# A wider padding tile under the experts' operand blocks: 256 bytes instead of 128

## The chip, the cores and the metric

The kernel runs on one core of a Trainium2 chip. The metric is the device time of one execution in microseconds (us); single matmuls are given in nanoseconds (ns). The engines are called as the profile calls them: PE is TensorE's matmul, PEld its weight load (the load of a matmul's stationary operand), DVE is VectorE, ACT is ScalarE, POOL is GpSimd, SP is SyncE, which issues most of the DMAs.

## The reference

Two stages follow each other. An attention over 8 batches, 8 heads, 576 positions and 64 values a head is the sum of a coarse attention over positions averaged by four and of a local one over a narrow band. Its output, 4608 tokens of 512 values, goes into a mixture of eight experts, in which every token goes to one expert:

```python
def _moe_ref(x, modality_id, w_gate, modality_bias, w1, w2):
    logits = x @ w_gate + modality_bias[modality_id]
    e_idx = np.argmax(logits, axis=1)
...
    gate_w = probs[np.arange(N), e_idx]
    for e in range(E):
        mask = e_idx == e
...
        h = np.maximum(x[mask] @ w1[e], 0.0)
        out[mask] = gate_w[mask, None] * (h @ w2[e])
```

Here w1 is 8 x 512 x 1024 and w2 is 8 x 1024 x 512, all in float32.

## The kernel before

**Two halves.** The first 238 us compute the attention and, with it, the routing: tokens are sorted by expert into a table in DRAM. From there on the kernel is a row of expert products, and the change touches only these.

**Units.** The loop over `order` (in `build`) goes through eight units of rows of one expert each: two of 512 rows (the early ones, "e"), three of 1024 rows ("q", class `Large`), then one of 256, one of 128 and one of 256 rows ("m"). A loop at the end takes what is left over, and on these inputs it runs no round. Every unit has a first product (rows by w1, then relu) and a second (hidden rows by w2, then a scale by the gate, then an indirect DMA to the output). Each number of an operand is split in two, a high part and a low part, and each product is three matmuls: high by high, low by high, high by low.

**Blocks.** An operand lives in a block of 8192 bytes in each of the 128 partitions: a high half and a low half of 4096 bytes, or, for rows of a unit of 512, one block for the high part and one for the low. `Moe.block` (the function that hands them out by name) takes them from pools. G0 and G1 come from the pool `xg`; G2, G3, H0 to H3, V2, V3 and raw2 from `mxb`; H4 and H5 from `mwa`; raw0 and raw1 from `mwr`. H6, H7, X0, X1, V0 and V1 come from `mwe`, which `open_early` opens on the right side, that is at the upper end of the memory:

```python
        s.we = ctx.enter_context(s.tc.tile_pool(name="mwe", bufs=1, side="right", reuse_waits="tile"))
```

A tile `pad` that nothing reads or writes is asked of this pool last, in `build`, just ahead of the loop over what is left. The pool ends at the memory's upper end, so the size of its last tile sets where the six blocks before it begin.

**Who meets whom on PE.** In a matmul one operand is stationary (loaded by PEld, 128 columns of 4 bytes) and one is moving (512 columns of 4 bytes, 256 in the first products of the units of 256 rows). Which blocks meet, by the code:

- Early units, first product (`compute`, L1003): weights in H4, H5, H6, H7 are stationary, rows in X0 and X1 are moving. 96 matmuls each, half of them with H4 and H5, half with H6 and H7.
- Early units, second product (`second`, L1057): hidden rows in H0 to H3 are stationary, weights in V0 to V3 are moving. 96 matmuls each.
- Large units, first product (`Large.first`, L1171): seven smaller products (three of eight are saved by sums, after Strassen and Winograd), whose operand blocks `Large.WHERE` lists, rows first, weights second. Of the first large unit:

```python
    WHERE = ({"1": "G0 G1", "2": "G2 G3", "5": "H4 H5", "6": "H6 H7", "7": "G0 G1", "4": "G2 G3", "3": "G0 G1"},
```

- In the other large units H2, H3, H0 and H1 stand in for H4 to H7, and for G0 to G3 in part. 168 matmuls a unit, 24 in each of the seven products. The raw rows, not yet split, are in X0 and X1, and only DVE, ACT and POOL read them there.
- Large units, second product (`second`, L1057): 192 matmuls a unit, 24 for each h of 0 to 7. In the first 12 of an h the moving weights are V0 and V1, in the last 12 V2 and V3. The hidden rows are stationary: for h of 0 to 3 H0 and H1 in the first 12 and H2 and H3 in the last 12, for h of 4 to 7 H4 and H5 and then H6 and H7.
- Units of 256 rows, first product (L1003): 96 matmuls each, weights in G and H blocks stationary, rows in X0 or X1 moving with 256 columns.
- Unit of 128 rows: first product (`compute_half`, L1025), 24 matmuls, rows in X stationary, weights in V0 to V3 moving; second product (L1057), 24 matmuls.

**What sets the order.** PE's order comes from the loops of `compute`, `Large.first` and `second` and from the framework's scheduler, which may put a ready matmul ahead; a unit's splits of weights and rows on ACT, DVE and POOL and the loads on SP's queue are hooked onto the matmuls, several to an h. Weights come as raw blocks over SP's queue (`fetch`, L849 and L852), are split by `wsplit` (L874 on ACT, L880 on DVE) or by `Large.split` (L1120 and L1121), rows come by indirect DMA on POOL's queue (L935) into `xg` tiles and are turned by PE (L963).

Of the kernel before, what the change touches and what calls it, by code (L numbers as in the profile page):

```python
# [7 lines left out]
F32 = mybir.dt.float32  # L8
# [1187 lines left out]
def build(tc, q, k, v, mid, w_gate, bias, w1, w2, out):  # L1196
    nc = tc.nc
    with ExitStack() as ctx:
# [9 lines left out]
        moe = Moe(tc, ctx, C, ps, xs, tab, w1, w2, out)  # L1208
# [350 lines left out]
                else:  # L1559
                    moe.compute(Ts[i], Ws[i], Xs[i], H, paced, mid, Js.get(i), i == N - 1)  # L1560

        moe.we.tile([128, 32], F32, name="pad")
        rbi, rei = ro.rest()
        nu = nc.values_load(rei[0:1, NLOOP : NLOOP + 1], min_val=0, max_val=NLOOP)  # L1564
        moe.after = ()
# [40 lines left out]
```

## Time and profile before

| what | value |
|---|---|
| median of 3 runs | 667.25 us (660.24 to 670.42) |
| profiled execution, whole time | 660.17 us |
| profiled execution, span of its instructions | 658.1 us |
| PE busy | 630.8 us, 96% of the span |
| DVE, ACT, POOL busy | 437.5, 384.4 and 341.9 us |
| DMA | 90.21 MB, mean 137 GB/s |

The span runs from the first to the last instruction of the core; the execution's own time has 2.1 us around it. A group of PE in the profile is 390 ns long for one matmul of 512 columns, since matmuls overlap; what one costs in a stream is the distance between the starts of neighbours.

### The profile page before, as it was taken

The page shows a single profiled execution, that of the slowest core. Times are in us where ns is not written, and L with a number is a line of the kernel's source. Part 1 is how long each engine was busy: PE and PEld are TensorE (multiplying, and loading weights), DVE is VectorE, ACT ScalarE, POOL GpSimd, SP SyncE. Part 2 cuts the span into 40 slices and gives each one's busy share as a digit, 9 for nine tenths or more (in the row PEclk, how much of TensorE's full clock was granted, in tenths as well). Part 3 has the DMA queues.
Part 4 walks back from the last instruction along what each step waited for, and adds up shares of the span by engine and source line. Part 5 has one row for each costly group of instructions (what it writes and reads, how often), then busy time and mean ns, then how long its engine had stood idle before and what let it go on. Part 6 is the DMA issues. An engine that isn't in the chain of part 4 may idle for free. (4 is left out here: it accounts for less than half of the span.)

```text
span 658.1 us, 16392 instructions
## 1 busy us (share of the span) xinstructions
PE 630.8 (96%) x6099; PEld 495.7 (75%) x6099; DVE 437.5 (66%) x896; ACT 384.4 (58%) x870; POOL 341.9 (52%) x378
## 2 busy tenths in 40 slices
PE   9899999999998889998999999999999999999996
PEld 5677676666766667876888788887888878889794
DVE  6689898899988866933456754567548775246610
ACT  4689989988998863212545623456234574245610
POOL 6644564745557861515078775588755721141211
PEclk9899999998999999999999999999999999999998
DMA  8999997899989975498012454134431345349300
GB/s 191 205 188 195 175 183 149 159 182 147 176 162 149 195 200 154 82 179 207 17 35 100 106 140 117 49 97 109 124 136 49 101 119 173 121 151 289 125 15 32
DMA packets 168860, 90.21 MB, mean 137 GB/s; under 512 B 131812, under 2 KB 153354, under 8 KB 168778
## 3 DMA queue, kind: packets, MB, share of 16 engines
q1 hardware_dynamic: 160810, 69.96, 50.3%
q0 software_dynamic: 7968, 19.18, 9.6%
q8 instruction: 49, 0.80, 0.6%
q14 instruction: 33, 0.27, 0.2%
HBM read 69.86 MB, written 19.51 MB: 136 GB/s over the span
## 5 line engine op out<-in xcount | busy, mean ns | idle before, releaser
L1057 PE MATMUL l<-V,H 128*128 128x512 f32 x792 | 187.2, 394 | 0.0
L1057 PEld LDWEIGHTS l<-V,H 128*128 128x128 f32 x792 | 148.0, 188 | 33.9
L943 POOL DMA_INDIRECT xg<-xs,m x64 | 77.0, 1204 | 19.2 <-issue 18.9
L426 POOL TENSOR_TENSOR le<-le,zr 128x384 f32<-128x384 f32 x32 | 26.6, 832 | 78.0 <-DVE zr L422 40.9
L1067 POOL DMA_INDIRECT out_dram<-o,tq x24 | 27.4, 1140 | 74.6 <-ACT o L1059 55.8
L1003 PE MATMUL l<-X,H 128*128 128x512 f32 (+1 forms) x240 | 54.2, 375 | 2.8 <-ACT o L1059 1.8
L442 ACT COPY Pw<-lt 32x288 f32<-32x288 f32 x128 | 54.6, 427 | 1.6
L1059 ACT ACTIVATE o<-l,tq 128x512 f32<-128x512 f32 x24 | 16.6, 690 | 66.5 <-issue 27.8
L640 POOL DMA_INDIRECT tab<-ig,si x36 | 36.8, 1022 | 26.1 <-DVE mni L662 18.1
L1003 PEld LDWEIGHTS l<-X,H 128*128 128x128 f32 x240 | 41.5, 188 | 11.3 <-ACT o L1059 2.2
L1160 ACT ACTIVATE H<-o 128x512 fp32r<-128x512 f32 x36 | 22.8, 634 | 39.6 <-DVE o L1182 30.2
L331 ACT COPY kT<-tp 64x512 f32<-64x512 f32 x64 | 37.2, 581 | 8.9 <-PE tp L294 7.4
L481 PEld LDWEIGHTS avl<-Pw,vw 128*64 128x64 f32 x768 | 32.7, 137 | 10.9 <-ACT Pw L442 3.4
L481 PE MATMUL avl<-Pw,vw 128*64 128x96 f32 x768 | 38.8, 250 | 2.2 <-ACT Pw L442 2.2
L1067 POOL DMA_INDIRECT out_dram<-o,tg x10 | 11.3, 1132 | 52.9 <-ACT o L1059 35.8
L880 DVE TENSOR_TENSOR V<-raw,V 128x1024 fp32r<-128x1024 f32 x22 | 31.8, 1467 | 10.2 <-ACT V L874 9.1
L1121 DVE TENSOR_TENSOR G<-X,G 128x1024 fp32r<-128x1024 f32 x15 | 23.2, 1551 | 22.3 <-ACT G L1120 16.1
L1009 DVE SCALAR_TENSOR_TENSOR H<-l,H 128x512 fp32r<-128x512 f32 x24 | 16.1, 686 | 32.7 <-ACT H L1008 28.6
L412 ACT ACTIVATE de<-scd,dm 128x144 f32<-128x144 f32 x96 | 35.2, 373 | 1.7 <-DVE dm L404 0.4
L373 PE MATMUL sc<-kT,qT 128*24 128x64 f32 x1536 | 35.1, 224 | 0.4 <-ACT qT L318 0.3
L1008 ACT ACTIVATE H<-l 128x512 fp32r<-128x512 f32 x24 | 13.9, 596 | 35.9 <-PE l L1003 27.8
L373 PEld LDWEIGHTS sc<-kT,qT 128*24 128x24 f32 x1536 | 24.7, 104 | 12.9 <-issue 10.5
(282 smaller groups left out, 1437.6 us busy)
## 6 DMA issues: line engine op xcount, KB each, us to landing
raw<-in_moe_w_dram SPq DMA_DIRECT2D x112, 128.0 KB
raw<-in_moe_w_dram SPq DMA_DIRECT2D x28, 512.0 KB
vw<-in_v_dram SPq DMA_DIRECT2D x60, 180.0 KB
qt<-in_q_dram SPq DMA_DIRECT2D x26, 288.0 KB
kt<-in_k_dram SPq DMA_DIRECT2D x26, 288.0 KB
xs<-R SPq DMA_DIRECT2D x48, 128.0 KB
xs<-G SPq DMA_DIRECT2D x16, 128.0 KB
qt<-in_q_dram SPq DMA_DIRECT2D x6, 256.0 KB
```

The source lines that it names most:

```text
L331: s.nc.scalar.copy(s.kB[r, g, a, PAD + 64 * g : PAD + 64 * g + 512], p[r])
L373: s.nc.tensor.matmul(p[32 * j : 32 * j + SUB, 2 * i : 2 * i + 2, :], qT[:, q0 : q0 + SUB], kB[:, :, q0 : q0 + WIN], start=False, stop=(i = ...
L412: s.nc.scalar.activation(x, s.t["scd", n][:, c].rearrange("p (k x) -> p k x", k=NB), AF.Exp, bias=m[:, c : c + 1], accum_out=s.t["z", n][: ...
L426: s.nc.gpsimd.tensor_tensor(e, e, z[:, : 2 * NB].unsqueeze(2).broadcast_to([128, 2 * NB, WIN]), op=ALU.mult)
L442: s.nc.scalar.copy(s.Pw[n % NPW][r, :, j, :SUB], s.t["lt", n][r, :, :SUB])
L481: s.nc.tensor.matmul(p[64 * a : 64 * a + 64, c], vw[:, NB * (4 * (hp // 2) + hp % 2 + 2 * a) + k, :], Pw[:, 2 * k + a], start=True, stop=T ...
L640: i = nc.gpsimd.indirect_dma_start(out=s.tab[:, :], out_offset=bass.IndirectOffsetOnAxis(ap=C.si[:, t : t + 1], axis=0), in_=C.ig[:, t, :] ...
L880: (nc.gpsimd if turn == 4 else nc.vector).tensor_tensor(lo, raw, hi.bitcast(F32), op=ALU.subtract)
L943: s.nc.gpsimd.indirect_dma_start(out=R[l].rearrange("p h (i x) -> p (h i) x", i=4)[:, i, :], out_offset=None, in_=s.xs.rearrange("n (a x) ...
L1003: nc.tensor.matmul(p[:, f % n, :], a[:, fs], x[:, k, :N], start=(k == 0 and i == 0), stop=(k == 3 and i == 2))
L1057: nc.tensor.matmul(p, l, x[:, f % 2, :], start=(f == 0 and i == 0), stop=(f == 7 and i == 2))
L1067: nc.gpsimd.indirect_dma_start(out=s.out[:, :], out_offset=bass.IndirectOffsetOnAxis(ap=T[:, h, 0:1], axis=0), in_=o, in_offset=None, boun ...
```

## The change

One number: the padding tile is 64 floats wide in each partition, not 32.

```diff
-        moe.we.tile([128, 32], F32, name="pad")
+        moe.we.tile([128, 64], F32, name="pad")
```

Every instruction stands where it stood, on every engine, with the same waits: the two programs differ in nothing but where six blocks begin. They move down by 128 bytes a partition. All other tiles keep their addresses, and no DMA reads or writes the six blocks. The places, in bytes from the start of a partition:

| blocks | pool | before | modulo 256 | after | modulo 256 |
|---|---|---|---|---|---|
| X0, X1 | `mwe` | 180064, 188256 | 96 | 179936, 188128 | 224 |
| H6, H7 | `mwe` | 196448, 204640 | 96 | 196320, 204512 | 224 |
| V0, V1 | `mwe` | 212832, 221024 | 96 | 212704, 220896 | 224 |
| raw0, raw1, H4, H5 | `mwr`, `mwa` | 24288 to 48864 | 224 | the same | 224 |
| G0, G1 (either place) | `xg` | 70880, 81120 | 224 | the same | 224 |
| V2, V3, H0, H2, H1, H3, G2, G3, raw2 | `mxb` | 99552 to 165088 | 224 | the same | 224 |

Slices of a block that a matmul takes begin at multiples of 512 bytes in it, so an operand has its block's offset modulo 256.

## Rows read from the trace of the kernel before

**Rows 1.** The page: the span, and PE's busy time, share and instructions.
```profile
span 658.1 us, 16392 instructions
...
PE 630.8 (96%) x6099; PEld 495.7 (75%) x6099; DVE 437.5 (66%) x896; ACT 384.4 (58%) x870; POOL 341.9 (52%) x378
```

**Rows 2.** Busy time by stretch (start:end, length, engines with instructions, PE clock, DMA).
```profile
238.00:302.00 64.00, 60.69 (x324) 47.18 (x324) 40.08 (x130) 19.41 (x34) 25.37 (x22) 1.00 0.71 159
302.00:651.50 349.50, 347.96 (x1632) 287.28 (x1630) 191.35 (x208) 159.62 (x222) 175.42 (x149) 1.00 0.37 108
...
383.40:424.20 40.80, 40.80 (x178) 33.04 (x177) 23.76 (x27) 15.72 (x19) 24.45 (x26) 1.00 0.41 110
...
591.10:603.00 11.90, 11.90 (x101) 11.86 (x101) 6.75 (x7) 6.31 (x9) 2.78 (x3) 1.00 1.01 315
...
614.00:629.00 15.00, 13.49 (x65) 10.67 (x64) 6.19 (x8) 6.85 (x10) 4.20 (x4) 1.00 0.10 36
```

**Rows 3.** PE's timeline (start, length, group), first large unit, first product.
```profile
341.29 5.60 PE L1171 MATMUL qx<-G 128*128 128x512 f32 x24
346.73 5.61 PE L1171 MATMUL qz<-G,G 128*128 128x512 f32 x24
352.17 1.31 PE L1171 MATMUL qx<-H,H 128*128 128x512 f32 x5
353.31 5.61 PE L1171 MATMUL qz<-H,H 128*128 128x512 f32 x24
358.76 4.48 PE L1171 MATMUL qx<-H,H 128*128 128x512 f32 x19
363.08 5.61 PE L1171 MATMUL qx<-G 128*128 128x512 f32 x24
```

**Rows 4.** PE's timeline, first large unit, second product, and what follows.
```profile
375.24 3.88 PE L1057 MATMUL l<-V,H 128*128 128x512 f32 x16
378.95 4.72 PE L1171 MATMUL qz<-G 128*128 128x512 f32 x20
...
383.51 40.95 PE L1057 MATMUL l<-V,H 128*128 128x512 f32 x176
424.29 0.40 PE L1171 MATMUL qx<-H,H 128*128 128x512 f32 x1
```

**Rows 5.** The same row of 176, cut at h of 1 (halves), 2, 3, 4, 5, 6.
```profile
390.87 2.96 PE L1057 MATMUL l<-V,H 128*128 128x512 f32 x12
393.66 2.90 PE L1057 MATMUL l<-V,H 128*128 128x512 f32 x12
396.40 5.69 PE L1057 MATMUL l<-V,H 128*128 128x512 f32 x24
401.93 5.75 PE L1057 MATMUL l<-V,H 128*128 128x512 f32 x24
407.51 5.75 PE L1057 MATMUL l<-V,H 128*128 128x512 f32 x24
413.11 5.75 PE L1057 MATMUL l<-V,H 128*128 128x512 f32 x24
```

**Rows 6.** PE's timeline, first unit of 256 rows, first product.
```profile
591.17 8.80 PE L1003 MATMUL l<-X,G 128*128 128x256 f32 x72
599.80 0.38 PE L963 MATMUL xt<-ident,xg 128*128 128x128 f32 x2
```

**Rows 7.** PE's and ACT's timelines, second early unit, first product (idle and releaser in brackets).
```profile
290.15 5.70 PE L1003 MATMUL l<-X,H 128*128 128x512 f32 x24
297.63 3.02 PE L1003 MATMUL l<-X,H 128*128 128x512 f32 x12 [1.78 <-ACT o L1059]
301.77 0.44 PE L963 MATMUL xt<-ident,xg 128*128 128x128 f32 x2 [1.12 <-issue]
...
290.66 1.05 ACT L1120 CAST G<-raw 128x1024 fp32r<-128x1024 f32 x1 [7.55 <-DMA raw<-in_moe_w_dram]
```

**Rows 8.** Groups by line and form on ACT: count, busy us, mean ns.
```profile
L1120 ACT CAST G<-raw 128x1024 fp32r<-128x1024 f32 x15 | 15.7, 1044 | 14.6 <-DMA raw<-in_moe_w_dram 7.5 <-DMA tq<-tab 3.7 <-DVE raw L1114 1.8
L1120 ACT CAST G<-X 128x1024 fp32r<-128x1024 f32 x15 | 15.5, 1041 | 0.0
```

## Prediction

> **What bounds the kernel now.** I read the page first: PE is busy for 630.8 of 658.1 us, no other engine for more than 66% [rows 1]. Next the stretches: from 302 to 651.5 us PE is busy for 347.96 of 349.50 us at a granted clock of 1.00, the upper of the two levels, 2.4 GHz [rows 2]. So there the matmuls themselves set the end, and a nanosecond less for each is a nanosecond less for the kernel as often as it occurs. Between 238 and 302 us it is less clear: 60.69 of 64.00 us [rows 2], with two visible waits near the end [rows 7].
>
> The third view decides this case: PE's timeline in the expert products. The instructions are all alike there (stationary 128x128, moving 128x512), so the distance between the starts of two rows, divided by the count of the first, compares pairs of blocks. By the table of addresses a pair is "equal" when both blocks begin at the same offset modulo 256 (224 with 224, or 96 with 96) and "unequal" when one is at 96 and the other at 224.
>
> - Equal at 224: product 1 of the first large unit (G0, G1), 346.73 - 341.29 = 5.44 us for 24, 226.7 ns each; product 5 (H4, H5), 358.76 - 353.31 = 5.45 us, 227.1 ns each [rows 3].
> - Equal at 96: product 6 (H6, H7), which PE takes in pieces of 5 and 19: 1.14 + 4.32 = 5.46 us, 227.5 ns each [rows 3].
> - Unequal throughout: the second product at h of 4 and more. The h that begins at 407.51 lasts until 413.11, 5.60 us for 24, 233.3 ns each [rows 5].
> - Half and half: h of 2, from 396.40 to 401.93, 5.53 us, 230.4 ns each. The h before it shows the halves: the 12 with V0 and V1 (unequal) take 2.79 us, 232.5 ns each, the 12 with V2 and V3 (equal) 2.74 us, 228.3 ns each [rows 5].
>
> So a stream of unequal pairs pays about 6 ns a matmul over one of equal pairs, a mixed stream 3.4 ns on the average (230.4 - 227), and it is the difference of the two offsets that pays, not the offset 96, since 96 with 96 is as quick as 224 with 224. After the change every pair of the expert products is equal.
>
> **The change part by part.** Nothing is added, removed or moved in any queue; the only term is what a matmul costs.
>
> 1. Large units, second product. The row of 176 lasts from 383.51 to 424.29, 40.78 us, 231.7 ns each; at 227 it lasts 39.95 us, 0.83 less. The 16 ahead of it take 3.71 us, 231.9 ns each, 0.08 more to gain [rows 4]. That is 0.91 us a unit and 2.7 us for the three, which are alike by the code.
> 2. Second early unit, second product: 96 matmuls, half unequal, 96 x 3.4 = 0.33 us. Its first product counts from 302 us on, 60 of its 96 matmuls: 0.2 us.
> 3. Last units: the unit of 128 rows has two products of 24 matmuls and the last unit a second product of 48, all half unequal by the blocks that meet: 96 x 3.4 = 0.33 us.
> 4. Units of 256 rows, first product: 192 matmuls of 256 columns, all unequal today. They take (599.80 - 591.17) / 72 = 119.9 ns each [rows 6], and here PEld is busy for 11.86 of 11.90 us [rows 2], so the weight load may be what sets the pace. The trace has no equal pair at 256 columns. Bounds: a gain of 6 ns each, as much as a matmul of 512 columns, is 1.15 us; on the other side the load may suffer, which is the third rival below. The nearest row is the 512-column one, and half its columns give half of it: 3 ns, 0.58 us. I take 0.5.
> 5. Ahead of 302 us: 228 matmuls of the early units, half unequal, 228 x 3.4 = 0.78 us. I count nothing of it. PE waits 1.78 us for ACT at 297.63 and 1.12 us at 301.77 for gathered rows; ACT in turn stood for 7.55 us until 290.66 for a DMA of raw weights [rows 7]. A PE that comes sooner there waits longer.
> 6. DVE, ACT and POOL also use the moved blocks. ACT's split takes 1044 ns from a raw block at 224 and 1041 ns from an X block at 96 [rows 8]: an address costs these engines nothing that shows. They also have cover: the busiest, DVE, works for 191.35 of the 349.50 us behind 302 [rows 2].
>
> Sum: 2.7 + 0.5 + 0.3 + 0.5 = 4.0 us (0.2 and 0.33 of point 2 taken together). The profiled execution would go from 660.17 to 656.2 us. That execution is at the lower end of the four that are known: 660.17, 660.24, 667.25 and 670.42, mean 664.5. The profiled one shows where time goes; the mean is what a new run is likely to stand against, so the forecast is 664.5 - 4.0 = 660.5 us. Against the median of the three runs shown, 667.25, it is 1% less, of which 0.6% is the change and the rest is the spread of the runs.
>
> The Trainium skill has a rule against the change. In "SBUF — State Buffer", section "Who interferes with whom", PE has two read ports of its own, one for the moving operand and one for weight loads, and these are called independent of each other. By that rule no offset between the two operands could matter and the sum would be nothing. The trace does not agree as it stands: 227 ns against 233 for the same instruction on different pairs.
>
> **The rivals.**
>
> *The offset is not the cause.* All unequal pairs of the trace are also pairs of one block of the upper pool with one below it, and all equal pairs lie on one side. If it is the place in the memory that pays, a shift of 128 bytes changes nothing: 664.5 us. For it: the trace has no pair that separates the two. Against it: the place alone costs nothing that shows, neither PE at H6 and H7 (227.5 ns [rows 3]) nor ACT [rows 8], and below it blocks at all distances meet at 227 to 228 ns (G0 and G1 10 KB apart, H4 and H5 8 KB, V2 and H2 24 KB). The Trainium skill's rule on the ports, above, stands with this rival.
>
> *The gain is given back.* PE arrives up to 3.5 us sooner at the last units, where it already waits: 13.49 busy of 15.00 us from 614 to 629 [rows 2], and DMA is at a share of 1.01 from 591 to 603. If the weights of the last units cannot come sooner, the gain of the last large unit and of all behind it is lost, 0.9 + 0.3 + 0.5 = 1.7 us: 662.2 us. Against it: the loads are hooked on steps of PE's own work and begin sooner with it, and from 591 to 603 PE itself never waits (11.90 of 11.90).
>
> *The weight load pays (slower).* An equal pair could be quick because the load stands back behind the moving operand. With 512 columns nobody sees this, since PEld is busy for 33.04 of 40.80 us only [rows 2]. With 256 columns PEld has no slack. At the worst load and matmul follow each other: half of 227 is 113.5, put on top of 119.9, for 192 matmuls 21.8 us, less the 3.5 gained elsewhere: 682.8 us. It outweighs the gain from 3.5 / 192 = 18 ns a matmul on. Against it: 256-column matmuls at 119.9 are slower today, not faster, than half of 233 (116.5), so being unequal shows no benefit that could be lost.
>
> **How the numbers follow.** Forecast (gain of 2.5 to 5.5 us): 0.62. Given back: 0.18. Not the cause: 0.10. The load pays: 0.06, of which about half goes past 2%. Left for a larger gain than any row supports: 0.04. Two per cent, 13 us, is about what a measurement of this kernel can tell from no change. To be faster by that would take 20 ns for each of the 672 unequal matmuls of 512 columns, where 6 are seen: 0.04. Slower by it: the bad half of the third rival, 0.03, and 0.01 for the spread: 0.04. Within 2%: 0.92. Range: the low end is the lowest run, 660.2, less 4.7 us (the sum and the rest of the bound of point 4), 655.5; the high end is the median of the runs with nothing gained, 667. It holds the first two rivals.
>
> **What would show it.** Right: in the profile after, an h of 4 or more of a large second product lasts 5.45 us instead of 5.60, the row of 176 about 40.0 instead of 40.8, the stretch from the first large unit's first matmul to the first of the next comes at 82.1 us instead of 83.0, and products 1, 5 and 6 stay at 227 ns. The 256-column matmuls come at 117 ns or near it. PE's waits around 297 to 302 us grow by about what the early units gain. Wrong: the row of 176 stays at 40.8 (not the cause), or it falls and the span does not (given back; then PE shows new idle time after 590), or the 72 matmuls of 256 columns take longer than 8.63 us (the load pays).

## The result and the profile after

| | before | after |
|---|---|---|
| median of 22 runs | 664.56 us | 658.24 us |
| lowest, mean, highest | 656.52, 664.1, 670.42 us | 652.94, 660.2, 675.21 us |
| profiled execution, its span | 660.17, 658.1 us | 658.49, 656.4 us |

The ratio is 0.9901, 95% interval 0.9872 to 0.9929: faster by 1%, clear of no change and well within 2%. The ratio takes in only the runs within 1.5% of the fastest of their own kernel, which leaves out eight of the 22 after; over all runs the two means are 3.9 us apart, a ratio of 0.994. The forecast was 660.5 us and a gain of 4.0 us.

First the rows that decide. The timeline of PE in the first large unit after the change, first product and then the row of 176 of the second product, and the same row cut into its blocks of 12 and 24 (columns as in [rows 3]):

```profile
342.60 5.60 PE L1171 MATMUL qx<-G 128*128 128x512 f32 x24
348.04 5.60 PE L1171 MATMUL qz<-G,G 128*128 128x512 f32 x24
353.48 1.29 PE L1171 MATMUL qx<-H,H 128*128 128x512 f32 x5
354.61 5.60 PE L1171 MATMUL qz<-H,H 128*128 128x512 f32 x24
360.05 4.47 PE L1171 MATMUL qx<-H,H 128*128 128x512 f32 x19
364.36 5.60 PE L1171 MATMUL qx<-G 128*128 128x512 f32 x24
...
384.68 40.06 PE L1057 MATMUL l<-V,H 128*128 128x512 f32 x176
424.58 0.39 PE L1171 MATMUL qx<-H,H 128*128 128x512 f32 x1
...
391.94 2.88 PE L1057 MATMUL l<-V,H 128*128 128x512 f32 x12
394.66 2.88 PE L1057 MATMUL l<-V,H 128*128 128x512 f32 x12
397.38 5.60 PE L1057 MATMUL l<-V,H 128*128 128x512 f32 x24
408.26 5.60 PE L1057 MATMUL l<-V,H 128*128 128x512 f32 x24
413.70 5.60 PE L1057 MATMUL l<-V,H 128*128 128x512 f32 x24
```

The row of 176 lasts 424.58 - 384.68 = 39.90 us, 226.7 ns a matmul, where it was 40.78 [rows 4]. The block that begins at 408.26 lasts 5.44 us, where its counterpart lasted 5.60 [rows 5], and the two blocks of 12, which took 2.79 and 2.74 us, now take 2.72 each. The first product is as it was (5.44 us for 24). So the second product now runs at the pace that only equal pairs had before.

Next the stretches. Of before, one for each large unit (from its first matmul to the next unit's first), columns as in [rows 2]:

```profile
341.29:424.29 83.00, 83.00 (x361) 67.43 (x360) 51.43 (x59) 38.54 (x54) 59.94 (x52) 1.00 0.36 99
424.29:507.30 83.01, 82.99 (x361) 67.41 (x360) 50.68 (x56) 38.78 (x54) 61.20 (x47) 1.00 0.35 105
507.30:591.17 83.87, 83.86 (x370) 68.16 (x369) 47.53 (x52) 40.44 (x57) 29.71 (x26) 1.00 0.43 126
...
228.10:235.00 6.90, 5.61 (x88) 4.20 (x88) 5.73 (x13) 6.37 (x19) 4.14 (x5) 1.00 0.86 205
```

The last row, and the last two of the next fence, show the stretch ahead of the experts in which the two executions differ. After the change:

```profile
342.60:424.58 81.98, 81.97 (x362) 67.42 (x360) 51.73 (x58) 38.52 (x54) 60.03 (x54) 1.00 0.38 103
424.58:506.80 82.22, 82.20 (x362) 67.60 (x361) 53.80 (x58) 38.68 (x54) 58.88 (x45) 1.00 0.36 103
506.80:589.52 82.72, 82.71 (x368) 67.97 (x367) 47.40 (x52) 40.48 (x57) 28.67 (x26) 1.00 0.45 127
...
224.00:228.10 4.10, 2.25 (x44) 1.51 (x36) 4.03 (x9) 3.77 (x14) 2.18 (x5) 1.00 0.71 166
228.10:235.00 6.90, 5.53 (x52) 3.98 (x53) 3.54 (x9) 2.74 (x10) 0.87 (x2) 0.51 0.95 232
```

The three large units take 246.92 us instead of 249.88, 2.96 less, with PE busy throughout in both. That is more than the two spans differ by (1.7 us), because the profiled execution after lost time ahead of the change. PE's timeline of before and then of after at that place (idle time and releaser in brackets):

```profile
228.57 1.06 PE L279 MATMUL vp<-vw,pool 128*32 128x256 f32 x12 [0.64 <-issue]
...
229.47 1.93 PE L279 MATMUL vp<-vw,pool 128*32 128x256 f32 x12 [2.40 <-DMA vw<-in_v_dram]
```

After, PE waits 2.40 us there for a DMA of v, and from 228 to 235 us its granted clock was 0.51, the lower of the two levels, 1.2 GHz, following a stretch in which PE was busy for 2.25 of 4.10 us. Before, no such fall stands there (a clock of 1.00 for the same stretch), and the first expert product begins at 238.41 us; after, it begins at 241.79. The account of the profiled pair is then: 3.4 us lost ahead of the experts, 1.76 less from there to the second early unit's restart (301.77 us in [rows 7], 303.39 after), 0.31 less from there to the first large unit, 2.96 less in the large units, 0.34 less in the last units, and 0.3 more behind the last matmul: 1.7 us less.

### The profile page after: what moved, and what is told of

It reads as the page before. It is cut to its first block, busy times and chain, and to the rows that moved or that the text cites. A ratio compares the mean times of both kernels' runs of the same rounds, so it can differ in the third digit from the quotient of the medians.

```text
span 656.4 us, 16392 instructions
## 1 busy us (share of the span) xinstructions
PE 628.5 (96%) x6099; PEld 496.8 (76%) x6099; DVE 438.6 (67%) x896; ACT 383.9 (58%) x870; POOL 338.5 (52%) x378
## 5 line engine op out<-in xcount | busy, mean ns | idle before, releaser
L1057 PE MATMUL l<-V,H 128*128 128x512 f32 x792 | 183.7, 390 | 0.0
L943 POOL DMA_INDIRECT xg<-xs,m x64 | 74.4, 1163 | 19.2 <-issue 19.2
L880 DVE TENSOR_TENSOR V<-raw,V 128x1024 fp32r<-128x1024 f32 x22 | 35.1, 1621 | 9.9 <-ACT V L874 9.7
```

The lines of the kernel that those rows point to most:

```text
L880: (nc.gpsimd if turn == 4 else nc.vector).tensor_tensor(lo, raw, hi.bitcast(F32), op=ALU.subtract)
L943: s.nc.gpsimd.indirect_dma_start(out=R[l].rearrange("p h (i x) -> p (h i) x", i=4)[:, i, :], out_offset=None, in_=s.xs.rearrange("n (a x) ...
L1057: nc.tensor.matmul(p, l, x[:, f % 2, :], start=(f == 0 and i == 0), stop=(f == 7 and i == 2))
```

## The experiments

Each kernel differs from before or after in addresses alone. The first four ran on one chip, beside 35 runs of the kernel before; their rows of 176 are the first large unit's, from its first start to the start that follows, and the granted clock over each of these rows, in every run below, was 1.00.

**again**: the changed kernel, unedited.

> The changed kernel once more. Offset theory (a pair of operands 128 bytes apart modulo 256 pays about 6 ns a matmul, and that is all the change does): the row of 176 matmuls of the first large second product lasts 39.9 us, and the time is 4 us under the kernel before, a ratio of 0.994. Rival (a second source outside the expert products makes the first comparison's 0.990): the ratio is 0.990 again and the stretch ahead of 238 us is shorter by 2 us in runs without a fall of the clock.

```profile
385.06 40.06 PE L1057 MATMUL l<-V,H 128*128 128x512 f32 x176
424.95 1.30 PE L1171 MATMUL qx<-H,H 128*128 128x512 f32 x5
```

The row lasts 39.89 us. The ratio is 0.9902 (0.9854 to 0.9950, 12 runs); the means are 665.0 and 661.7 us, 3.3 apart. The stretch ahead of 238 us holds falls of the clock in every profile so far (in this one at 21 and at 215 us), at places that change from execution to execution, so no profile so far can show the 2 us that the rival asked for; those of the later kernels can (at the end of the next section). Every run lists its mean granted clock, and a straight line through time and clock of both kernels' runs, with one slope, takes the clock out: the changed kernel lies 2.9 us (plus or minus 1.6, two standard errors) under the one before. This speaks for the offset theory and a gain of 3 to 4 us; the ratio by itself says more (taken up below).

**all96**: the first pool's padding shifts all lower blocks to 96.

```diff
-        pool.tile([128, 48], F32, name="pad")
+        pool.tile([128, 80], F32, name="pad")
```

> The padding of the first pool is 128 bytes larger, the upper pool stands as before: all blocks of the experts begin at 96 modulo 256. Offset theory: the row of 176 lasts 39.9 us instead of 40.8, the tail's half-unequal products come at 227 ns, and the time is that of the changed kernel, 0.994. Place theory (blocks of the upper pool pay when they meet lower ones, wherever they begin): 40.8 us and no gain. Tiles of the attention shift too, so if its time depends on their offsets the stretch ahead of 238 us differs.

**swap**: both paddings enlarged.

```diff
-        pool.tile([128, 48], F32, name="pad")
+        pool.tile([128, 80], F32, name="pad")
...
-        moe.we.tile([128, 32], F32, name="pad")
+        moe.we.tile([128, 64], F32, name="pad")
```

> Both paddings enlarged: the lower blocks at 96, the upper ones at 224 modulo 256. Offset theory: unequal pairs again, the row of 176 lasts 40.8 us and an h of 4 or more 5.60 us, the time is that of the kernel before, 1.000, although both changes are in. If 224 in the upper pool were what helps: 39.9 us and 0.994.

**pad96**: the upper blocks 256 bytes lower.

```diff
-        moe.we.tile([128, 32], F32, name="pad")
+        moe.we.tile([128, 96], F32, name="pad")
```

> The upper pool's padding is 384 bytes: its six blocks stand 256 bytes lower than before, at 96 modulo 256 as before. Offset theory with 256 as the modulus: as before, 40.8 us for the row of 176, ratio 1.000. If a wider padding or a lower place helps by itself: 39.9 us or less, 0.994.

The rows of 176 with the starts that follow, of all96:

```profile
394.96 40.05 PE L1057 MATMUL l<-V,H 128*128 128x512 f32 x176
434.86 4.24 PE L1171 MATMUL qx<-H,H 128*128 128x512 f32 x18
```

of swap:

```profile
385.02 40.95 PE L1057 MATMUL l<-V,H 128*128 128x512 f32 x176
425.81 4.28 PE L1171 MATMUL qx<-H,H 128*128 128x512 f32 x18
```

and of pad96:

```profile
390.88 40.95 PE L1057 MATMUL l<-V,H 128*128 128x512 f32 x176
431.67 4.28 PE L1171 MATMUL qx<-H,H 128*128 128x512 f32 x18
```

| kernel | lower, upper blocks modulo 256 | row of 176 | ratio (interval) | us under before at one clock |
|---|---|---|---|---|
| again | 224, 224 | 39.89 us | 0.9902 (0.9854 to 0.9950) | 2.9 ± 1.6 |
| all96 | 96, 96 | 39.90 us | 0.9949 (0.9899 to 0.9999) | 3.5 ± 1.5 |
| swap | 96, 224 | 40.79 us | 0.9955 (0.9915 to 0.9995) | -0.3 ± 1.5 |
| pad96 | 224, 96 | 40.79 us | 0.9949 (0.9902 to 0.9997) | -0.4 ± 1.6 |

This settles the cause. With no edit to the upper pool, all96 has the whole gain; with both edits, swap has none; a shift of 256 bytes does nothing. Place, width of the padding and the offset 224 itself are out; what counts is that the two operands begin alike modulo 256. It also warns of times alone: by their ratios swap and pad96 are 0.5% faster than before as well, though their rows of 176 and their large units are not, and in the column at one clock they are not either.

**pad56, pad48, pad40**: other distances between the two offsets.

```diff
-        moe.we.tile([128, 32], F32, name="pad")
+        moe.we.tile([128, 56], F32, name="pad")
```

(48 and 40 in the other two.)

> Upper blocks at 0 modulo 256, 32 bytes from the lower ones at 224. If any difference of the offsets pays in full: the row of 176 lasts 40.8 us and an h of 4 or more 5.60 us. If the cost grows with the distance up to 128 bytes: about 40.1 and 5.48. If differences within 64 bytes are free: 39.9 and 5.44.

> Upper blocks at 32 modulo 256, 64 bytes from the lower ones. Any difference pays: 40.8 us for the row of 176, 5.60 for an h of 4 or more. Growing with the distance: 40.3 and 5.52. If 64 bytes were the modulus: 39.9 and 5.44.

> Upper blocks at 64 modulo 256, 96 bytes from the lower ones. Any difference pays: 40.8 us for the row of 176, 5.60 for an h of 4 or more. Growing with the distance: 40.6 and 5.56.

PE's timeline of pad56, the row of 176 and the first product of the first unit of 256 rows:

```profile
386.73 41.06 PE L1057 MATMUL l<-V,H 128*128 128x512 f32 x176
427.62 4.26 PE L1171 MATMUL qx<-H,H 128*128 128x512 f32 x18
...
594.70 8.57 PE L1003 MATMUL l<-X,G 128*128 128x256 f32 x72
603.11 0.38 PE L963 MATMUL xt<-ident,xg 128*128 128x128 f32 x2
```

| bytes between the offsets | row of 176 | 72 matmuls of 256 columns, ns each |
|---|---|---|
| 0 (after) | 39.90 us | 120.0 |
| 32 (pad56) | 40.89 us | 116.8 |
| 64 (pad48) | 40.72 us | 117.8 |
| 96 (pad40) | 40.98 us | 120.0 |
| 128 (before) | 40.78 us | 119.9 |

For 512 columns any difference pays, and about in full: nothing grows with the distance, and 32 bytes are as bad as 128. For 256 columns it is another way round: equal and 128 apart are alike, and 32 apart is the quickest. The times (one run each, 663.46, 656.42 and 657.20 us, beside 656.34 to 664.55 before) tell nothing.

**midshift**: the changed kernel, with 128 bytes put at the start of one of the lower pools.

```diff
-        s.xb = ctx.enter_context(tc.tile_pool(name="mxb", bufs=1, reuse_waits="tile"))
+        s.xb = ctx.enter_context(tc.tile_pool(name="mxb", bufs=1, reuse_waits="tile")); s.xb.tile([128, 32], F32, name="pad")
```

> The changed kernel with 128 bytes of padding at the start of the pool of G2, G3, H0 to H3, V2, V3 and raw2, which so begin at 96 modulo 256, while G0, G1, H4, H5 and the upper six stay at 224. Offset theory: the cost comes back at other places: in a large second product now V0 and V1 pay with H0 and H1 (h of 0 to 3) and V2 and V3 with H6 and H7 (h of 4 to 7), so every h is half unequal, 5.53 us, and the row of 176 lasts 176 x 230.4 = 40.55 us; an h of 4 or more, where only blocks of the upper and lower pools met at a cost before, has an equal half. Place theory: as in the changed kernel, 39.9. The 256-column matmuls meet G0 and G1 equally, G2, G3 and H blocks unequally: 120 ns either way, as measured in both kernels. Time: 1.7 us above the changed kernel, too little for the comparison of times to settle.

The row lasts from 384.28 to 424.81, 40.53 us. Four of its blocks of 12, the first and third with V0 and V1 moving, the others with V2 and V3:

```profile
391.65 2.96 PE L1057 MATMUL l<-V,H 128*128 128x512 f32 x12
394.45 2.90 PE L1057 MATMUL l<-V,H 128*128 128x512 f32 x12
...
408.23 2.90 PE L1057 MATMUL l<-V,H 128*128 128x512 f32 x12
410.96 2.95 PE L1057 MATMUL l<-V,H 128*128 128x512 f32 x12
413.76 5.46 PE L1057 MATMUL l<-V,H 128*128 128x512 f32 x23
```

By the starts they take 2.80 us (V0 and V1 at 224 with H0 and H1 at 96) and 2.73 (both at 96), later 2.73 (V0 and V1 with H4 and H5, all at 224) and, to the next block's start at 413.76, 2.80 (V2 and V3 at 96 with H6 and H7 at 224). The cost went where the table of offsets sent it: all three pairs of an upper with a lower block paid before and none did after, and here the two with unequal offsets pay and V0 and V1 with H4 and H5, equal again, do not. Time 0.9968 (0.9914 to 1.0022), four runs, which tells nothing, as expected.

**best**: what both tables ask for at once (the edit is against the changed kernel).

```diff
-        s.turn = {}
+        s.turn, s.skew = {}, 0
...
+        if nm in ("X0", "X1"):
+            return pool.tile([128, 2112], dt, name=nm)[:, s.skew : s.skew + 2048]
         return pool.tile([128, 2048], dt, name=nm)
...
+            s.skew = 8 if H == 2 else 0
             t = s.block(f"X{k % 2}")
+            s.skew = 0
...
-        moe.we.tile([128, 64], F32, name="pad")
```

> All blocks at 224 modulo 256 and no padding tile (the pool then ends where its blocks are at 224 anyway); X0 and X1 are 256 bytes longer, and the units of 256 rows begin 32 bytes into them, so that the moving rows stand at 0 and the stationary weights at 224. Theory (512 columns want equal offsets, 256 columns want 32 bytes between them): the 72 matmuls of 256 columns ahead of the first interruption come at 117.2 ns, 8.44 us instead of 8.63, the row of 176 stays at 39.9 us, and the two first products of 96 together gain 0.5 us on the changed kernel. Rival (the 117 ns with 32 bytes between them came from something else that the shift of all six blocks did): 120 ns. Time: 3.5 to 4.5 us under the kernel before, 0.9935; the half microsecond over the changed kernel is less than a comparison of times can tell.

PE's timeline of best (its lines are numbered 2 to 4 higher than before's):

```profile
379.72 40.05 PE L1061 MATMUL l<-V,H 128*128 128x512 f32 x176
419.61 4.24 PE L1175 MATMUL qx<-H,H 128*128 128x512 f32 x18
...
584.61 8.57 PE L1007 MATMUL l<-X,G 128*128 128x256 f32 x72
593.02 0.38 PE L965 MATMUL xt<-ident,xg 128*128 128x128 f32 x2
```

The row of 176 takes 39.89 us and the 72 matmuls 8.41 us, 116.8 ns each: both as expected, so it is the 32 bytes between rows and weights, and not the shift of H6, H7, V0 and V1, that quickens the 256-column product. Ratio 0.9936 (0.9911 to 0.9962, 12 runs), at one clock 4.0 ± 1.3 us under before. Its profiled span is the shortest of all, 651.2 us. Of the half microsecond over the changed kernel only a part arrives: the two first products of 256 columns take 11.58 and 11.20 us instead of 11.87 and 11.51, 0.6 less, but between them PE waits 0.59 us for ACT (in the unit of 128 rows, `ht`) where it waited 0.30, so the last units as a whole are 0.3 us shorter. The times cannot tell this from nothing.

**pad0**: before without its padding tile.

```diff
-        moe.we.tile([128, 32], F32, name="pad")
+        pass
```

> The padding tile is left out: the six blocks stand 128 bytes higher than before, at 224 modulo 256. Offset theory: the row of 176 lasts 39.9 us, as in the changed kernel. If it is the width of the padding that helps: 40.8 us or more.

```profile
380.69 40.06 PE L1057 MATMUL l<-V,H 128*128 128x512 f32 x176
420.58 4.24 PE L1171 MATMUL qx<-H,H 128*128 128x512 f32 x18
```

From 380.69 to 420.58, 39.89 us (one run, 654.46 us, beside 655.11 to 662.97 before). The pool's end already puts its blocks at 224; the padding tile of before is what took them off. Here the upper blocks stand 256 bytes higher than in the changed kernel and are as quick, so 256 holds as the modulus for equal pairs as pad96 showed it for unequal ones.

## Why the prediction was right

The forecast holds: 660.5 us was said, 658.24 is the median and 660.2 the mean; a gain of 4.0 us was said, and the profiled pair shows 3.6 us from 302 us on (0.31 + 2.96 + 0.34). The mechanism is the one that was said. That the sum came so near is in part luck: point 4 put in 0.5 us that did not come and point 2 0.2 too much, against 0.26 too little in point 1, and the 664.5 us it was taken from was the mean of four runs that lie 10 us apart (of all 22 it is 664.1). Point by point:

1. *Large units, second product, 2.7 us.* Measured 2.96. The pace came out at 226.7 ns, not the 227 that I rounded to, and the equal blocks that followed unequal ones (228.3 ns) recovered too. One label was off by one: the row of 176 begins inside h of 0, so what the prediction and the heading of [rows 5] call h of 1 and 2 are 2 and 3. The blocks' pairs, and the sum, are the same.
2. *Second early unit, 0.5.* Measured 0.31, from 301.77 to 341.29 before and from 303.39 to 342.60 after.
3. *Last units, 0.33.* Measured 0.34, from the first matmul of 256 columns to the end of the last row of PE.
4. *256 columns, 0.5.* Wrong: nothing. PE's timeline after:

```profile
589.52 8.79 PE L1003 MATMUL l<-X,G 128*128 128x256 f32 x72
598.16 0.38 PE L963 MATMUL xt<-ident,xg 128*128 128x128 f32 x2
```

The 72 take from 589.52 to 598.16, 8.64 us, where they took 8.63 [rows 6]. The step that failed is that half the columns give half the gain. These matmuls do not follow the 512-column rule at all; of the five distances that were run, 32 bytes between the operands is their quickest, and why is not shown. The two other sides of the bound fell as well: they neither gained as much as the long ones, nor did the load pay (third rival; 0.01 us is as fine as the starts are given).
5. *Ahead of 302 us, nothing counted.* The profiled pair shows 1.76 us less, and most of it, 1.23 us, is not the matmuls': PE came 3.4 us later to a place that waits for a DMA, and waited less. About half a microsecond is theirs: the first early unit's second product takes 22.26 us (270.90 to 293.16) instead of 22.58 (267.57 to 290.15), and the 24 behind it 0.1 less. PE's row and ACT's after:

```profile
299.31 3.02 PE L1003 MATMUL l<-X,H 128*128 128x512 f32 x12 [0.55 <-ACT o L1059]
303.39 0.44 PE L963 MATMUL xt<-ident,xg 128*128 128x128 f32 x2 [1.07 <-DMA xg<-xs,tq]
...
292.50 1.05 ACT L1120 CAST G<-raw 128x1024 fp32r<-128x1024 f32 x1 [9.30 <-DMA raw<-in_moe_w_dram]
```

PE's wait of 1.78 us at 297.63 [rows 7] is 0.55 here, while ACT still stands for the DMA, 9.30 us. So this place is a buffer: it takes back part of what is lost ahead of it. That it takes what is gained there as well fits the other profiles: from the first expert product to the first large unit they need 100.1 to 101.2 us with equal offsets (again, all96, best, pad0) and 100.5 to 101.1 with unequal ones (swap, pad96, pad56, pad48, pad40); the 102.88 of before is the longest of all. The prediction's sign (PE's waits there grow) was not seen in the pair, since the delay ahead of it went the other way and was larger.
6. *Other engines, nothing.* Nothing seen: after, ACT is busy for 383.9 us in all, before 384.4, and its split from the X blocks, now at 224, takes 1042 ns, where it took 1041 [rows 8].

The rival that the offset is not the cause is refuted by all96, swap and pad96. That the gain is given back at the last units is refuted in the profiled pair, where they gain what was said. Where the Trainium skill ("SBUF — State Buffer", "Who interferes with whom") calls PE's two read ports independent, these runs differ: 226.7 ns against 233.3 [rows 5] for one instruction, by nothing but the start of its operands. What happens inside PE that makes it so no row shows.

What stays open is the rest of the ratio: 0.990 twice is 6.5 us, the rows have 3.6, and swap and pad96, with no gain in those rows, still came out at 0.995. The profiles show no second source. The three large units together take 246.9 to 247.0 us in after, best and pad0 (248.3 and 248.1 in again and all96, with the stop described below) and 249.7 to 250.6 in before, swap, pad96, pad56, pad48 and pad40. Ahead of them every profile has a fall of the clock, but five have none from 162 to 238 us, and in these the first expert product begins at 236.46 and 238.12 us with equal offsets (best, pad0) and at 238.41, 237.23 and 236.31 with unequal ones (before, pad48, pad40): the 2 us that the rival of again asked for are not there. In the other seven it begins at 241.8 us or later, with offsets of either kind. Over all runs, too, the means are 3.9 and 3.3 us apart, not 6.5. Since the spread of the runs goes with the granted clock, and taking it out leaves 2.9 to 4.0 us for kernels with the gain and nothing for those without, I hold the rows' size to be the change's; that a second source adds to the times now and then is not excluded.

## What to carry to other kernels

In a stream of 512-column float32r matmuls that PE alone bounds, look also at the starts of both operands modulo 256: the same instruction took 226.7 ns with equal offsets and about 6 more at 128 bytes apart, with nearly the same toll at 32, 64 and 96, and a padding tile or its removal sets it. Compare starts in the timeline between groups of the same instruction on different buffers; the kernel before already showed the two paces, and what it could not show, whether the place or the offset sets them, took two kernels with other paddings (all96 and swap). Where a change is worth half a per cent, judge it by such rows and by runs at one clock, since times alone called two kernels without any gain half a per cent faster.

## What the runs showed that was not expected

The 256-column matmuls are quickest with 32 bytes between the offsets (116.8 ns), not with none (120.0).

The toll outlasts the pair that pays it. In an equal half behind an unequal one in before (the 12 from 393.66), the first three matmuls still start 231 to 232 ns apart and only the rest 226 to 227, which is why such a half has 228.3 on the average. With 64 bytes between the offsets (pad48) the same halves take 2.77 us, 230.8 ns on the average, as much as the unequal halves beside them.

In two of the profiles with equal offsets, again and all96, PE lost 1.3 and 1.2 us at one place in the second large unit's second product (its row of 176 lasts 41.21 and 41.05 us). PEld's timeline of again there, with idle time and releaser in brackets:

```profile
478.82 0.41 PEld L1057 LDWEIGHTS l<-V,H 128*128 128x128 f32 x2 [0.25 <-issue]
479.56 0.30 PEld L1057 LDWEIGHTS l<-V,H 128*128 128x128 f32 x2 [0.34 <-issue]
480.32 0.19 PEld L1057 LDWEIGHTS l<-V,H 128*128 128x128 f32 x1 [0.46 <-issue]
481.04 1.11 PEld L1057 LDWEIGHTS l<-V,H 128*128 128x128 f32 x5 [0.53 <-issue]
```

No semaphore held it ("issue"). The DMA queues between 478 and 481.5 us show what shared them:

```profile
q1 hardware_dynamic: 268, 0.56, 64.1%
q0 software_dynamic: 54, 0.12, 12.4%
q8 instruction: 1, 0.02, 1.7%
```

One packet of instructions moves in that time beside a heavy load of weights on q1. That PE had run out of instructions and waited for this packet fits, but was not tried, and the packet alone does not stop PE: after has one on q8 between 470 and 492 us as well. Other profiles, after's and before's among them, have no such stop there.
